# A block kernel's instruction order, written out anew, and a builder that keeps no times

## The chip, the cores and the metric

The kernel runs on one core of a Trainium2 chip. The metric is the device time of one execution in microseconds. The core has five instruction queues that run side by side and wait for each other through semaphores: PE (TensorE), ACT (ScalarE), DVE (VectorE), POOL (GpSimd) and SP (SyncE, which here only starts transfers).

## The reference

A transformer block with sliding-window attention and a gated MLP, both behind a layer norm that is modulated by a condition vector `c`. 2048 tokens, width 640, 32 heads of 20, window 256, MLP width 1536, all in bf16:

```python
mod = (silu(c) @ w_mod).reshape(1, 6, 1, -1)        # sa, ca, ga, sb, cb, gb
h = layernorm(x) * (1 + ca) + sa
q, k, v = heads(h @ wqkv)
p = softmax(where(0 <= i - j < 256, q @ k.T * 20 ** -0.5, -1e9))
x = x + ga * ((p @ v) @ wo)
h = layernorm(x) * (1 + cb) + sb
x = x + gb * ((sigmoid(h @ w_gate) * (h @ w_up)) @ w_down)
```

## The kernel before

The 2048 tokens are cut into eight blocks `a` of 256. For each block the program has these steps; the tag is the name that this document uses.

- `ln1`: load of x, layer norm (DVE statistics, a power on POOL, the normalisation on DVE or POOL), a transpose to `hT` (on PE for the first three blocks, by a transposing transfer on SP after that), and the modulation with scale and shift on DVE, ACT or POOL.
- `qkv`: q, k and v projections in 480-column pieces, five matmuls each. Copies on ACT or DVE bring them out of PSUM to `stg` (q, k) and `V`. q and k are then transposed to `QT` and `KT`, on PE for blocks 0 and 1 and by transfers on SP from block 2 on.
- `score_set`: scores of four heads at a time, one set after another into the one PSUM buffer `S` (four banks). ACT takes `exp` of them into `E` (L1015). A block has two halves of 16 heads, and a half has four "main" sets and one "edge" set (block 0 has other sets). POOL cuts the window's edges out of `E` (`masks`, L1040).
- `burst` and `norm`: the product with V (PV) for 16 heads into two PSUM tiles; DVE transposes them, divides by the row sums and transposes back. Eight small transfers write the result to a scratch tensor (`doc`), two read it back as `oT`.
- `outproj`: product with `wo`, the sum with x, the second layer norm, two transposing transfers to `h2T`, the modulation.
- `mlp`: gate and up products in pairs of 512 columns, tanh on ACT (L1209), the product `hh` on DVE (L1211), then the down projection, the sum with x, and the store.

The gates `ga` and `gb` are multiplied into `wo` (L1253) and `wd` (L1192) once; for each a row goes through a scratch tensor (`gate`) and is broadcast back to `gbc` by a transfer. The parts of `w_mod` first lie in the places of `wd`, `wu` and `hh`.

All matmuls but the small-tile ones are issued in one helper line (L668), the small-tile ones (scores, PV, the modulation rows) in another (L669). All products but the scores share four PSUM banks, `p_M`.

The order is not made by the program's text. Each of the 2121 operations gets a whole number from the table `PRIO`: divided by five it is the operation's rank in one common order, and the rest names its engine (0 PE, 1 ACT, 2 DVE, 3 POOL, 4 SP). `Prog.schedule` goes through the operations by rank, appends each to its engine's queue, gives each tile a buffer of its pool when its first operation comes, and `Prog.emit` writes the queues and the semaphore waits. Before, `schedule` also kept a model of times (start and end of each operation, of the transfers, of a port that DVE and POOL share), and took the buffer that by the model came free first:

```python
rts = [slot_time(t.pool, s + k) for k in range(step)]
if None not in rts and (best is None or max(rts) < best[0]):
    best = (max(rts), s)
```

Two tiles that are "mates" get neighbouring buffers.

Of the kernel before, what the change touches and what calls it, by code (L numbers as in the profile page):

```python
# [25 lines left out]
SWITCH = 0.095  # L26
ENGATTR = {"pe": "tensor", "act": "scalar", "dve": "vector", "pool": "gpsimd", "sp": "sync"}
ENGS = ("pe", "act", "dve", "pool", "sp")
OVERLAP = {"pe": 0.0, "act": 0.085, "dve": 0.075, "pool": 0.045, "sp": 0.0}
# [52 lines left out]
class Prog:  # L82
# [69 lines left out]
    def schedule(self):  # L152


        free = {e: START for e in ENGS}
        bw = 0.0
        lastturn = False
# [4 lines left out]
        pemode = 0  # L162
        portend = 0.0
        freed = {}

        def slot_time(pool, s):
            ten = pool.tenant[s]
            if ten is None:
                if not all(x.done for x in pool.init[s]):
                    return None  # L170
                return max([x.end + x.lat for x in pool.init[s]], default=0.0)
            return None if ten.left else freed[ten]
# [7 lines left out]
        for o in sorted(self.ops, key=lambda x: x.prio):  # L180
# [4 lines left out]
            st = max([o.tmin, free[e] + (SWITCH if e == "pe" and o.mode != pemode else 0.0)]  # L185
                     + [d.end + (0.0 if d.eng == "pe" and e == "pe" else d.lat) for d in o.deps])
            if o.isdma and e == "sp":
                st = max(st, bw - QMAX)
            for t in o.tiles:
                if t.slot is None:  # L190
                    step = 1 if t.mate is None else 2
                    best = None
                    for s in range(0, len(t.pool.tenant), step):
                        rts = [slot_time(t.pool, s + k) for k in range(step)]
                        if None not in rts and (best is None or max(rts) < best[0]):
                            best = (max(rts), s)
# [6 lines left out]
                for x in t.prev:  # L203
                    st = max(st, x.end + x.lat)
            if e == "dve" and o.port:
                st = max(st, free["pool"])
            elif e == "pool":
                st = max(st, portend)
            o.start = st
            if e == "pe":  # L210
                pemode = o.mout
            dur = o.dur[e]
            free[e] = st + dur - OVERLAP[e]
            if e == "dve" and o.port:
                portend = free[e]
            if o.isdma:
                turn = o.dlat > 3.0
                if e == "sp" and bw - st > 2.0:
                    free[e] += 0.35 if o.dur[e] > 1.0 else 0.1
                bw = max(st + o.dlat, bw + (MIXED if turn != lastturn and bw > st + o.dlat else 0.0)) + o.work  # L220
                lastturn = turn
                o.end = max(bw - 0.83, st + dur)
                s = rr
                rr = (rr + 1) % NDMA
                dmacnt[s] += 16
                o.key, o.val = f"d{s}", dmacnt[s]
                if dmalast[s] is not None:
                    o.deps.append(dmalast[s])
                dmalast[s] = o
            else:  # L230
                o.end = st + dur
# [16 lines left out]
        self.span = max(o.end for o in self.ops)  # L248
# [88 lines left out]
def c_pe(n):  # L337
# [3 lines left out]
PE_EPS = 0.14  # L341
PRIO = [
# [121 lines left out]
PQ = ()  # L464
KEEP = 3
DSAFE = 1.5
START = 0.8
PORTLAG = 0.05
MIXED = 0.55
NPB = 0  # L470
# [836 lines left out]
```

## Time and profile before

| | |
|---|---|
| median of 3 runs | 326.33 us (325.88 to 327.26) |
| span of the profiled execution, first to last instruction | 324.3 us |
| the profiled execution's own time | not listed; the three runs lie 1.6 to 3.0 us above the span |
| granted TensorE clock | 1.000 |
| PE, weight loads, DVE, ACT, POOL busy | 317.3, 222.7, 211.8, 212.3, 187.2 us |
| transfers | 37.85 MB, 117 GB/s over the span |

The row of a stretch has its bounds and length, then for PE, weight loads, DVE, ACT and POOL the busy time and the number of instructions, then the granted clock, the transfers' share and GB/s. A row of a timeline has its start, its length, the engine, the line, the operation, outputs and inputs, the count, and in brackets the idle time before it and what ended it. A row of the chain of waits has start, length and what ran or was waited for. PE's lengths overlap, since matmuls are pipelined: the next one starts before the last one's end.

### The profile page before, as it was taken

The page shows a single profiled execution, that of the slowest core. Times are in us where ns is not written, and L with a number is a line of the kernel's source. Part 1 is how long each engine was busy: PE and PEld are TensorE (multiplying, and loading weights), DVE is VectorE, ACT ScalarE, POOL GpSimd, SP SyncE. Part 2 cuts the span into 40 slices and gives each one's busy share as a digit, 9 for nine tenths or more (in the row PEclk, how much of TensorE's full clock was granted, in tenths as well). Part 3 has the DMA queues.
Part 4 walks back from the last instruction along what each step waited for, and adds up shares of the span by engine and source line. Part 5 has one row for each costly group of instructions (what it writes and reads, how often), then busy time and mean ns, then how long its engine had stood idle before and what let it go on. Part 6 is the DMA issues. An engine that isn't in the chain of part 4 may idle for free.

```text
span 324.3 us, 11594 instructions
## 1 busy us (share of the span) xinstructions
PE 317.3 (98%) x4872; PEld 222.7 (69%) x4873; DVE 211.8 (65%) x424; ACT 212.3 (65%) x316; POOL 187.2 (58%) x276
## 2 busy tenths in 40 slices
PE   8999999989999999999999999999999999999997
PEld 3564545446776568765776467877786788787885
DVE  5797898778687959674477475837463769264332
ACT  1899985889876687788687867786767764011120
POOL 5128869976668694847585939382939691012100
DMA  7998799989891383824405394340213032202101
GB/s 249 371 333 299 165 269 180 200 137 183 260 164 22 83 109 77 152 61 101 85 22 82 97 103 110 92 69 5 81 40 88 3 79 53 76 20 64 40 2 40
DMA packets 71694, 37.85 MB, mean 117 GB/s; under 512 B 45274, under 2 KB 70362, under 8 KB 71642
## 3 DMA queue, kind: packets, MB, share of 16 engines
q1 hardware_dynamic: 69616, 35.31, 48.3%
q10 hardware_dynamic: 2026, 1.80, 2.1%
q8 instruction: 38, 0.62, 0.8%
q14 instruction: 14, 0.11, 0.1%
HBM read 21.30 MB, written 5.25 MB: 82 GB/s over the span
## 4 chain that ended last, share of the span: by engine, by line
PE 73%; DMA 2%; SPq 2%; DVE 1%; POOL 1%; issue 0%; DVEq 0%
PE M L668 61%; PE S L669 6%; PE M L669 5%; DMA gbc<-gate 2%; SPq L803 2%; DVE wd L1192 1%; POOL x L793 0%; POOL st L788 0%; DVE hh L1211 0%; POOL E L1040 0%; DVE x L1230 0%; DVEq L310 0%
## 5 line engine op out<-in xcount | busy, mean ns | idle before, releaser
L1040 POOL TENSOR_SCALAR_AFFINE_SELECT E<-E 128x512 bf16<-128x512 bf16 (+1 forms) x176 | 142.6, 836 | 68.7 <-ACT E L1015 67.0
L1015 ACT ACTIVATE E<-S 128x512 bf16<-128x512 f32 (+2 forms) x184 | 150.9, 878 | 47.4 <-PE S L669 46.5
L668 PE MATMUL M<-wqkv,hT 128*128 128x480 bf16 (+1 forms) x340 | 73.9, 355 | 0.6 <-ACT hT L846 0.5
L668 PE MATMUL M<-h2T,wu 128*128 128x256 bf16 x480 | 68.0, 273 | 0.5 <-DVE hh L1211 0.5
L668 PE MATMUL M<-h2T,wg 128*128 128x256 bf16 x480 | 67.8, 273 | 0.0
L668 PE MATMUL M<-wd,hh 128*128 128x320 bf16 (+2 forms) x396 | 58.1, 295 | 0.0
L1209 ACT ACTIVATE sig<-M 128x512 f32<-128x512 f32 x48 | 28.9, 602 | 44.1 <-PE M L668 41.7
L1211 DVE SCALAR_TENSOR_TENSOR hh<-sig,M 128x512 bf16<-128x512 f32 x48 | 32.4, 681 | 37.1 <-ACT sig L1209 24.0
L668 PEld LDWEIGHTS M<-h2T,wu 128*128 128x128 bf16 x480 | 45.9, 98 | 8.4 <-issue 1.2
L668 PEld LDWEIGHTS M<-h2T,wg 128*128 128x128 bf16 x480 | 45.7, 98 | 7.1
L668 PEld LDWEIGHTS M<-wqkv,hT 128*128 128x128 bf16 x340 | 30.1, 98 | 27.6 <-DMA wqkv<-in_A_wqkv_dram 1.6
L668 PEld LDWEIGHTS M<-wd,hh 128*128 128x128 bf16 x396 | 36.8, 98 | 14.3 <-DVE hh L1211 0.2
L669 PEld LDWEIGHTS S<-QT,KT 20*64 20x64 bf16 (+1 forms) x1856 | 19.9, 100 | 21.3 <-ACT E L1015 12.0
L1230 DVE TENSOR_TENSOR x<-M,x 128x320 bf16<-128x320 f32 (+2 forms) x33 | 15.6, 476 | 27.2 <-PE M L668 27.2
L669 PE MATMUL S<-QT,KT 20*64 20x256 bf16 (+5 forms) x1856 | 32.1, 228 | 1.2 <-ACT E L1015 1.2
L776 DVE BATCH_NORM_STATS2 st<-x 128x6 f32<-128x320 bf16 x64 | 28.6, 477 | 2.3 <-DMA x<-in_A_x_dram 1.9
L1082 DVE STREAM_TRANSPOSE T<-M 128x512 f32<-128x512 f32 x32 | 21.5, 698 | 9.2 <-PE S L669 8.0
L668 PE MATMUL M<-wo,oT 128*128 128x320 bf16 x160 | 25.4, 299 | 0.0
L669 PE MATMUL M<-E,V 128*32 128x128 bf16 (+1 forms) x960 | 22.8, 246 | 0.8 <-ACT E L1015 0.4
L781 POOL TENSOR_SCALAR st<-st 128x2 f32<-128x2 f32 x16 | 3.7, 234 | 33.8 <-DVE st L778 33.6
L669 PEld LDWEIGHTS M<-E,V 128*32 128x32 bf16 x960 | 19.2, 97 | 5.3 <-issue 2.9
L1091 DVE STREAM_TRANSPOSE On<-Tn 128x1024 bf16<-128x1024 bf16 x16 | 19.8, 1240 | 0.3
(77 smaller groups left out, 240.2 us busy)
## 6 DMA issues: line engine op xcount, KB each, us to landing
x<-in_A_x_dram SPq DMA_DIRECT2D x23, 160.0 KB, 2.3
doc<-On SPq DMA_DIRECT2D x56, 40.0 KB
wd<-in_B_w_down_dram SPq DMA_DIRECT2D x4, 480.0 KB
wd<-in_w_mod_dram SPq DMA_DIRECT2D x5, 320.0 KB
wqkv<-in_A_wqkv_dram SPq DMA_DIRECT2D x4, 400.0 KB
wu<-in_w_mod_dram SPq DMA_DIRECT2D x5, 320.0 KB
oT<-doc SPq DMA_DIRECT2D x8, 192.0 KB, 2.5
out_dram<-x SPq DMA_DIRECT2D x9, 160.0 KB
```

The source lines that it names most:

```text
L668: return e.matmul(o, l, r, start=st, stop=sp, skip_group_check=True)
L669: return e.matmul(o, l, r, start=st, stop=sp, tile_position=tp, skip_group_check=True)
L776: A("dve", lambda e, g, bi=bi, j=j: e.bn_stats(v(bi * 12 + j * 6, 6), src[bi].ap[:, j * 320:(j + 1) * 320]), 0.48, reads=[src[bi].r()], wr ...
L781: A("pool", lambda e, g: e.tensor_scalar(v(28, n), var(), EPS, None, op0=ALU.add), 0.2, reads=[st.r(("m", bi)) for bi in range(n)], writes ...
L803: return e.dma_start_transpose(dst(), src())
L1015: A("act", lambda e, eng: e.activation(dst(), src(), ACT.Exp, scale=SM_SCALE), c_act(n), reads=[Sp.r()], writes=[E.r(key)], prio=3, tag=f" ...
L1040: A("pool", lambda e, eng: e.affine_select(rows(dst), rows(src), pattern=[[0, 8], [sign, n]], compare_op=ALU.is_ge, fill=0.0, base=base, c ...
L1082: A("dve", lambda e, g, h=h: e.transpose(T1.ap[:, 512 * h:512 * h + 512], X[h].ap), 0.694, reads=[X[h].r()], writes=[T1.r(h)], prio=3.5, t ...
L1091: A("dve", lambda e, g: e.transpose(On.ap[:], Tn.ap[:]), 1.22, reads=[Tn.r()], writes=[On.r()], prio=4, tag=f"tr2_{a}")
L1209: A("act", lambda e, g, pg=pg, sg=sg: e.activation(sg.ap[:], pg.ap[:], ACT.Tanh, scale=0.5), c_act(512), reads=[pg.r()], writes=[sg.r()], ...
L1211: A("dve", lambda e, g, pu=pu, sg=sg, f0=f0: e.scalar_tensor_tensor(out=hh.ap[:, f0:f0 + 2, :], in0=sg.ap[:].rearrange("p (a b) -> p a b", ...
L1230: A("dve", lambda e, g, ps=ps, bi=bi, c0=c0, n=n: e.tensor_tensor(x1[bi].ap[:, c0:c0 + n], ps.ap[:, 0:n], x1[bi].ap[:, c0:c0 + n], op=ALU. ...
```

## The change

`PRIO` has new numbers for all operations except those at the first 150 ranks. 98 operations change their engine: PE keeps its 907 operations and SP its 193; ACT has 335 in place of 333, DVE 427 in place of 424, POOL 259 in place of 264. The matmuls are the same, in another order.

`schedule` keeps no times any more. A buffer is chosen by the rank at which its last tenant's last operation stood, in place of the modelled time at which it came free; what the next tenant waits for is each engine's last operation by rank, in place of by modelled start. The two PSUM tiles of a PV burst are no longer mates (`TR1` is 2 here), so they may lie in any two banks.

```diff
-SWITCH = 0.095
-OVERLAP = {"pe": 0.0, "act": 0.085, "dve": 0.075, "pool": 0.045, "sp": 0.0}
...
-        free = {e: START for e in ENGS}
-        bw = 0.0
...
-        def slot_time(pool, s):
+        def slot_rank(pool, s):
             ten = pool.tenant[s]
             if ten is None:
-                if not all(x.done for x in pool.init[s]):
-                    return None
-                return max([x.end + x.lat for x in pool.init[s]], default=0.0)
+                return -1 if all(x.done for x in pool.init[s]) else None
             return None if ten.left else freed[ten]
...
-        for o in sorted(self.ops, key=lambda x: x.prio):
+        for rank, o in enumerate(sorted(self.ops, key=lambda x: x.prio)):
...
-                        rts = [slot_time(t.pool, s + k) for k in range(step)]
-                        if None not in rts and (best is None or max(rts) < best[0]):
-                            best = (max(rts), s)
+                        ranks = [slot_rank(t.pool, s + k) for k in range(step)]
+                        if None not in ranks and (best is None or max(ranks) < best[0]):
+                            best = (max(ranks), s)
...
                 if t.left == 0:
+                    freed[t] = rank
                     last = {}
-                    for x in t.ops:
-                        if x.isdma:
-                            last[x] = x
-                    for e2 in ENGS:
-                        xs = [x for x in t.ops if x.eng == e2 and not x.isdma]
-                        if xs:
-                            last[e2] = max(xs, key=lambda x: x.start)
+                    for x in sorted(t.ops, key=lambda x: x.prio):
+                        last[x if x.isdma else x.eng] = x
                     t.rel = list(last.values())
-                    freed[t] = max(x.end + x.lat for x in t.rel)
...
 PRIO = [
-    23, 28, 258, 8, 43, 33, 958, 18, 1448, 38, 3, 507, 513, 72, 67, 48, 53, 58, 76, 84, 101, 99, 144, 149, 154, 159,
+    23, 28, 258, 8, 43, 33, 773, 18, 958, 38, 3, 507, 513, 72, 67, 48, 53, 58, 76, 84, 101, 99, 144, 149, 154, 159,
...
         X = [Tile(p_M, f"O{a}_{q}x"), Tile(p_M, f"O{a}_{q}y")]
-        X[0].mate, X[1].mate = X[1], X[0]
+        if TR1 == 1:
+            X[0].mate, X[1].mate = X[1], X[0]
```

Around the places that matter later, the new order on SP has the four loads of `wd` among the first transfers (ahead of the first gate's broadcast and of the reading back of block 0), the bulk loads of the second halves of `wg` and `wu` behind the transposes of block 2's and 3's q and k, and the second gate's broadcast directly ahead of those bulk loads.

More of the change, by code (lines that the diff above doesn't have):

```diff
@@ L152, in schedule @@
     def schedule(self):
-        free = {e: START for e in ENGS}
-        bw = 0.0
-        lastturn = False
         order = {e: [] for e in ENGS}
@@ L161, in schedule @@
         rr = 0
-        pemode = 0
-        portend = 0.0
         freed = {}
-        def slot_time(pool, s):
+        def slot_rank(pool, s):
             ten = pool.tenant[s]
             if ten is None:
-                if not all(x.done for x in pool.init[s]):
-                    return None
-                return max([x.end + x.lat for x in pool.init[s]], default=0.0)
+                return -1 if all(x.done for x in pool.init[s]) else None
             return None if ten.left else freed[ten]
@@ L184, in schedule @@
             o.eng = e
[L185 to L188, printed above, removed]
             for t in o.tiles:
@@ L202, in schedule @@
                         take(t.mate, best[1] + 1 - t.odd)
[L203 to L215, printed above, removed]
-            if o.isdma:
[L217 to L223, printed above, removed]
-                rr = (rr + 1) % NDMA
[L225 to L231, printed above, removed]
+            if o.isdma:
+                dmacnt[rr] += 16
+                o.key, o.val = f"d{rr}", dmacnt[rr]
+                if dmalast[rr] is not None:
+                    o.deps.append(dmalast[rr])
+                dmalast[rr] = o
+                rr = (rr + 1) % NDMA
             order[e].append(o)
@@ L236, in schedule @@
                 if t.left == 0:
+                    freed[t] = rank
                     last = {}
-                    for x in t.ops:
-                        if x.isdma:
-                            last[x] = x
-                    for e2 in ENGS:
-                        xs = [x for x in t.ops if x.eng == e2 and not x.isdma]
-                        if xs:
-                            last[e2] = max(xs, key=lambda x: x.start)
+                    for x in sorted(t.ops, key=lambda x: x.prio):
+                        last[x if x.isdma else x.eng] = x
                     t.rel = list(last.values())
-                    freed[t] = max(x.end + x.lat for x in t.rel)
         self.order = order
-        self.span = max(o.end for o in self.ops)
     def emit(self):
@@ L338, in c_pe @@
     return max(n, 64) / 2400.0 + 0.0027
-PE_EPS = 0.14
 PRIO = [
[3 rows of a table removed]
[3 rows of a table added]
     92, 87, 187, 237, 242, 247, 253, 263, 272, 267, 280, 275, 290, 300, 305, 286, 317, 296, 322, 311, 376, 357, 386,
[1 row of a table removed]
[1 row of a table added]
     541, 495, 501, 665, 677, 480, 485, 491, 565, 570, 576, 545, 551, 630, 652, 525, 555, 561, 625, 660, 681, 685,
[111 rows of a table removed]
[111 rows of a table added]
 ]
@@ L466 @@
 DSAFE = 1.5
-START = 0.8
-PORTLAG = 0.05
-MIXED = 0.55
 NPB = 0
@@ L484 @@
 WSE = (("dve", "pool"), ("dve", "pool"))
-QMAX = 4.5
 WDT = 72.0
```

228 rows, old and new, of the table PRIO are left out of this document.

## The prediction

> **What bounds the kernel now.** I read the page first, then the busy time by stretches, then PE's timeline where a stretch is not full, then the chain of waits and the queues behind each gap.
>
> ```profile
> span 324.3 us, 11594 instructions
> PE 317.3 (98%) x4872; PEld 222.7 (69%) x4873; DVE 211.8 (65%) x424; ACT 212.3 (65%) x316; POOL 187.2 (58%) x276
> ...
> 0.00:10.00 10.00, 8.35 (x76) 4.11 (x77) 5.56 (x19) 2.62 (x6) 4.73 (x25) 1.00 0.81 269
> ...
> 30.00:40.00 10.00, 9.65 (x166) 5.63 (x164) 9.13 (x18) 9.56 (x17) 7.50 (x12) 1.00 0.64 172
> ...
> 60.00:70.00 10.00, 8.85 (x111) 4.00 (x108) 7.78 (x18) 9.29 (x15) 8.69 (x12) 1.00 0.92 180
> 70.00:80.00 10.00, 9.58 (x190) 6.19 (x189) 9.09 (x16) 8.21 (x14) 6.72 (x10) 1.00 1.03 171
> 80.00:90.00 10.00, 9.49 (x165) 7.91 (x168) 6.57 (x12) 8.66 (x15) 6.31 (x8) 1.00 0.82 253
> 90.00:120.00 30.00, 30.00 (x514) 19.60 (x503) 23.82 (x54) 20.89 (x30) 23.45 (x32) 1.00 0.47 87
> ```
>
> PE is busy for 317.3 of 324.3 us. From 90 us it has no idle time that shows (30.00 of 30.00). The changed kernel has the same 907 PE steps, with the same matmuls in them, so nearly all of this stays. An order can win only the gaps of the first 90 us and the price of changes between kinds of matmul. The first 10 us hold 1.65 us of idle, but the first 150 operations keep their places, so that is not in play. What is in play is 30 to 90 us; there ACT and DVE are close to full beside PE (9.56 and 9.13 of 10).
>
> PE's "busy" holds modelled ends, so I measure stalls from start to start. First the prices of PE work, and the place at 32 to 38 us:
>
> ```profile
> 32.42 0.40 PE L669 MATMUL S<-QT,KT 20*128 20x128 bf16 x16
> ...
> 38.23 0.84 PE L669 MATMUL M<-E,V 128*32 128x256 bf16 x32 [0.35 <-DVE hT L858]
> 39.00 1.19 PE L668 MATMUL M<-wqkv,hT 128*128 128x480 bf16 x5
> 40.12 0.43 PE L669 MATMUL S<-QT,KT 20*64 20x256 bf16 x24
> ...
> 42.99 3.21 PE L668 MATMUL M<-wqkv,hT 128*128 128x480 bf16 x15
> 46.13 0.43 PE L669 MATMUL S<-QT,KT 20*64 20x256 bf16 x24
> ...
> 33.61 4.23 POOL L1040 TENSOR_SCALAR_AFFINE_SELECT E<-E 128x1024 bf16<-128x1024 bf16 x4 [2.01 <-ACT E L1015]
> 37.08 1.45 DVE L858 TENSOR_SCALAR hT<-M,mA 128x256 bf16<-128x256 f32 x3
> ```
>
> Fifteen 480-wide matmuls up to a score set take 46.13 - 42.99 = 3.14 us, five take 40.12 - 39.00 = 1.12 us. So one costs (3.14 - 1.12) / 10 = 0.202 us, and what is left, 0.11 us, is the change of kind.
>
> Then the largest gap, 58 to 71 us, PE and the ACT work between:
>
> ```profile
> 58.92 0.41 PE L669 MATMUL S<-QT,KT 20*128 20x64 bf16 x32
> 59.27 1.39 PE L668 MATMUL M<-wqkv,hT 128*128 128x480 bf16 x6
> 60.49 0.84 PE L668 MATMUL M<-wo,oT 128*128 128x320 bf16 x5
> 61.60 0.43 PE L669 MATMUL S<-QT,KT 20*64 20x256 bf16 x24 [0.27 <-ACT E L1015]
> 61.96 0.58 PE L668 MATMUL M<-wqkv,hT 128*128 128x480 bf16 x2
> 62.38 0.84 PE L668 MATMUL M<-wo,oT 128*128 128x320 bf16 x5
> 63.06 0.77 PE L668 MATMUL M<-wqkv,hT 128*128 128x480 bf16 x3
> 64.13 0.43 PE L669 MATMUL S<-QT,KT 20*64 20x256 bf16 x24 [0.30 <-ACT E L1015]
> 64.66 2.82 PE L668 MATMUL M<-wqkv,hT 128*128 128x480 bf16 x12
> 67.91 0.43 PE L669 MATMUL S<-QT,KT 20*64 20x256 bf16 x24 [0.42 <-ACT E L1015]
> 68.26 1.79 PE L668 MATMUL M<-wqkv,hT 128*128 128x480 bf16 x8
> 70.48 1.50 PE L669 MATMUL M<-E,V 128*32 128x128 bf16 x64 [0.42 <-ACT E L1015]
> ...
> 59.49 2.06 ACT L1015 ACTIVATE E<-S 128x512 bf16<-128x512 f32 x4 [0.72 <-PE S L669]
> ...
> 63.97 2.07 ACT L811 ACTIVATE hT<-hT,mA 128x256 bf16<-128x256 bf16 x4
> ```
>
> There is one buffer of scores, S. A score set writes it, ACT takes the exponentials out, and only then may the next set start. With ACT free this cycle takes 2.53 us (61.60 to 64.13) for a main set and 2.68 us (58.92 to 61.60) for the edge set. Whatever PE has to do between two sets beyond that hides it; less leaves a stall. A 320-wide matmul costs 0.136 us (five from 62.38 to 63.06), a set 0.36 us (61.60 to 61.96). The four distances of this place against their work: 2.68 against 0.35 + 6 x 0.202 + 5 x 0.136 + 0.1 = 2.34; 2.53 against 0.36 + 5 x 0.202 + 5 x 0.136 + 0.1 = 2.15; 3.78 against 0.36 + 12 x 0.202 + 0.1 = 2.88 (here four modulations, 2.07 us, stand on ACT ahead of the exponentials); 2.57 against 0.36 + 8 x 0.202 + 0.1 = 2.08. Lost: 0.34 + 0.38 + 0.90 + 0.49 = **2.1 us**.
>
> The last gap, at 86 us, is a transfer's:
>
> ```profile
> 73.62 4.26 SPq L803
> 77.92 5.14 DMA gbc<-gate
> ...
> 85.72 0.69 DVE hh L1211
> ...
> 84.78 1.26 PE L668 MATMUL M<-h2T,wg 128*128 128x256 bf16 x10
> 86.54 1.25 PE L668 MATMUL M<-h2T,wu 128*128 128x256 bf16 x10 [0.51 <-DVE hh L1211]
> ```
>
> The broadcast of the second gate stood on SP behind a transpose whose issue took 4.26 us, and landed 5.14 us after its own start. The scaling of wd waited for it at the head of DVE's queue, the products hh behind that, and PE behind those: **0.5 us**.
>
> **The change part by part.** The builder without times gives no instruction another cost. It only fills the buffers by the rank at which they came free, and the two PV outputs of a burst need no longer be neighbours. 98 operations change their engine: ACT gets 2 operations more, DVE 3 more, POOL 5 fewer, which no full PE stretch notices.
>
> *Changes of kind.* Walking PE's order, I count 162 changes between full-array matmuls and the smaller tilings before, 159 after: 3 x 0.11 = **-0.3 us**. The Trainium skill (TensorEngine Tiling (Array Packing), Key Properties) says that changing the tiling mode drains TensorE; the 0.11 us above agree, and by that rule too fewer changes is a gain.
>
> *The score cycle at 50 to 71 us.* In the new order PE stands like this (matmuls between sets, from the program):
>
> ```
> edge set, wqkv 480 x10, main set, wo 320 x17, main set, wqkv 480 x4, wo 320 x3, wqkv 480 x6,
> main set, wqkv 480 x15, PV + main set, wqkv 480 x10, edge set, wqkv 480 x15, main set
> ```
>
> The distances are 0.35 + 10 x 0.202 + 0.1 = 2.47 us after the edge set (needs 2.68: 0.2 lost), 0.36 + 17 x 0.136 + 0.1 = 2.77, 0.36 + 10 x 0.202 + 3 x 0.136 + 0.1 = 2.89, 0.36 + 15 x 0.202 + 0.1 = 3.49, and more than that to the end of the stretch. All but the first are over 2.53. ACT now has two modulations in place of four before one set, and three copies before the next, where PE has 3.49 us of cover or more. So 2.1 becomes 0.2: **-1.9 us**. Bounds: -2.1 if the edge set finds ACT early, -1.0 if the copies that now stand before the exponentials are late themselves.
>
> *The second gate.* Its broadcast now stands on SP right after the transposes of block 2 and 3, where PE is near 60 us of its work and not near 70, and ten us of PE work lie between it and the first scaling of wd. Three quarters of wd's transfers go out before 40 us and the last before 50. The 0.5 us go: **-0.5**. If that cover failed too, it would be 0.
>
> *The second PV of block 0 (38.23 us before).* This gets tighter. Before, 38.23 - 32.42 = 5.8 us lie between the second score set and the PV; in that time the four masks on POOL take 4.23 us from 33.61 to 37.84, and the wait that ended last was a copy out of PSUM (hT, 0.48 us each of three). In the new order the PE work between them is 0.34 + 8 x 0.202 + 22 transposes of 128 columns at 0.202 x 128 / 480 = 0.054 + 0.8 for the modulation rows (20 of 320 columns, four at a time: 5 x 0.136 and a change) + a main set of 0.36 = 4.3, and with four more changes 4.7 us. The masks cannot end sooner than 33.61 - 32.42 + 4.23 = 5.4 us after the set. So 0.7 us are lost at the PV where 0.5 were, and the next score set is only 1.7 us of work behind the last one, on ACT's 2.53: together with the PSUM banks that the transposed copies hold I take **+0.5 us**, between 0 and +1.5. Three of block 1's transposes are now put in one row at 16 us, with one bank too few: **+0.2**, between 0 and 0.4.
>
> *The last transpose of K of block 2.* Its source leaves PE 6.7 us of PE work before the first score set of block 2 that reads it; before, 11.4 us. In between stand four edge exponentials and a copy on ACT, two transposes of hT on SP, and its own.
>
> ```profile
> 292.52 2.53 SPq L803 DMA_TRANSPOSE h2T<-x  x2
> ...
> 298.13 2.71 POOL L812 TENSOR_SCALAR h2T<-h2T,scB,shB 128x256 bf16<-128x256 bf16 x5 [6.48 <-issue]
> 302.10 1.15 PE L668 MATMUL M<-h2T,wu 128*128 128x256 bf16 x9
> ```
>
> An issue takes 2.53 / 2 = 1.27 us, and the reader of the second one started 298.13 - 293.79 = 4.3 us after that issue began. Counted from the end of the K chain on PE: ACT is held to 1.4 us by the edge set, the copy ends at 2.0, SP is free of hT's transposes at 2.7, landing at 7.0: 0.3 late, and 0.4 of stall elsewhere cover it. **+0.1**, between 0 and +4 (a jammed issue as at 73.62).
>
> *The end.* Before the last MLP, PE has, by the same prices, 11.1 us of work behind the last output projection in place of 13.9. The modulations that ran from 298.13 to 300.84 on POOL alone, 1.3 us ahead of need at 302.10, are now on ACT and POOL; the transposes go out later by one product. **+0.1**, 0 to +1. The last 6.5 us of down projection and the final stores stay.
>
> Sum: -0.3 - 1.9 - 0.5 + 0.5 + 0.2 + 0.1 + 0.1 = **-1.8 us**. The profiled span of 324.3 becomes 322.5. The three runs have a median of 326.33, 2.0 above the span; the same distance gives **324.5 us**. About 0.5% (1.6 us) is what a measurement of this kernel can tell from no change; the forecast lies just beyond it.
>
> **The rivals.** *The gain stays small.* ACT and DVE are at 9 of 10 from 30 to 50 us; work that they did in the gap at 60 now stands earlier, and four PSUM banks are shared by copies, PV and projections. If the place at 33 us costs its upper bound and the score cycle gains only 1.0: -0.3 - 1.0 - 0.5 + 1.5 + 0.4 + 0.1 + 0.1 = +0.3, so 326.0 to 326.6. For it: 9.56 and 9.13 of 10. Against it: from 42 us on each distance between sets is over its cycle but one.
>
> *Slower: SP's order.* SP issues in order. If one transpose ahead of K's last takes 4.26 us as at 73.62 instead of 1.27, that landing is 3.0 us later and stands 3.3 us behind PE. It decides from 6.7 us after the chain's end. Price +3.3 + the rest = -1.8 + 3.3 = +1.5, or 327.9; with a second one jammed 330. For it: the cover was nearly halved. Against it: the bulk loads of wg and wu have moved behind this point. The Trainium skill (TensorE: Matmul & The Clock Gate, part 1) says that an idle window of about 3.4 us takes the clock down to half; the granted clock was 1.00 in all rows here, and by that rule a stall of that length would cost up to 1.7 us more.
>
> *It does not do what it says:* 98 operations move, but the gaps only change places: 326.3, as for a small gain.
>
> **How the numbers follow.** The forecast gets 0.50 (its bounds, -1.0 to -3.2, mostly over 0.5%), small or no gain 0.27, SP's order and other new waits 0.23. The range goes from -3.5 (all bounds at their good end, and 0.5 us of the small waits) to +2.1: 322.8 to 328.4. The forecast's own range is 323.1 to 325.3. Faster by over 0.5% 0.50, within 0.27, slower 0.23.
>
> **What would show it.** PE near 9.9 of 10 in 60 to 90 us, no wait of S for E over 0.3 us there, no wait of wd's scaling for gbc, and a stall of about 1 us ahead of the second PV of block 0. A wait of a score set of block 2 for a transposed K, or PE under 9.4 in any ten us after 20, would prove it wrong.

## The result, and the profile after

The changed kernel is slower, by less than half a per cent. In the first comparison it takes 327.60 us (median of 6 runs, 326.83 to 328.36) against 326.11 us (6 runs, 325.86 to 327.26) of the kernel before; the ratio is 1.0048, with a 95% interval of 1.0032 to 1.0064. Two later comparisons gave 1.0027 (1.0013 to 1.0041) and 1.0025 (1.0014 to 1.0036). Forecast was 324.5 us.

The page of the kernel after, and its busy time by stretches: length of the stretch, then busy us and instructions of PE, PEld, DVE, ACT and POOL, then the granted clock, DMA share and GB/s. Line numbers are 45 or 46 lower than before (PE's L668 is now L622).

```profile
span 326.0 us, 11592 instructions
PE 316.8 (97%) x4872; PEld 222.4 (68%) x4873; DVE 216.5 (66%) x427; ACT 213.4 (65%) x318; POOL 183.6 (56%) x271
...
0.00:10.00 10.00, 7.83 (x76) 3.67 (x77) 5.44 (x18) 2.50 (x6) 4.72 (x25) 1.00 0.78 257
...
30.00:40.00 10.00, 9.31 (x166) 5.29 (x164) 9.44 (x21) 9.42 (x16) 7.34 (x9) 1.00 0.94 226
60.00:70.00 10.00, 10.00 (x177) 5.66 (x176) 9.52 (x24) 7.97 (x13) 8.56 (x13) 1.00 0.83 211
70.00:80.00 10.00, 8.92 (x129) 5.26 (x127) 7.49 (x15) 7.37 (x11) 7.28 (x10) 1.00 1.08 200
80.00:90.00 10.00, 10.00 (x201) 8.45 (x183) 7.56 (x14) 8.71 (x13) 6.44 (x8) 1.00 0.73 151
90.00:120.00 30.00, 29.88 (x470) 19.73 (x468) 24.66 (x54) 23.22 (x34) 21.23 (x29) 1.00 0.55 97
120.00:150.00 30.00, 29.63 (x530) 20.62 (x529) 21.19 (x37) 21.61 (x33) 20.49 (x31) 1.00 0.27 63
150.00:180.00 30.00, 29.27 (x538) 21.41 (x537) 18.33 (x32) 21.66 (x32) 18.89 (x26) 1.00 0.43 80
270.00:300.00 30.00, 29.08 (x292) 23.10 (x291) 16.20 (x31) 5.87 (x10) 3.97 (x8) 1.00 0.37 66
```

PE is busy for 316.8 us in place of 317.3, but idle for 9.2 in place of 7.0. Read against the rows of before, 60 to 70 and 80 to 90 us are now full: they had 1.15 and 0.51 us of idle. Three losses stand against that. From 70 to 80 us, 1.08 us are idle in place of 0.42. In the first 10 us, where both kernels run the same operations, it is 2.17 in place of 1.65. And the part behind 90 us, which I had taken to be full, has 0.12 + 0.37 + 0.73 + 0.92 = 2.1 us of idle in the four rows shown; before, each of the four had 30.00 of 30.00. The rows of the kernel before that the prediction does not show:

```profile
120.00:150.00 30.00, 30.00 (x518) 21.72 (x516) 22.20 (x39) 22.70 (x33) 18.30 (x25) 1.00 0.55 97
150.00:180.00 30.00, 30.00 (x562) 21.73 (x561) 17.95 (x34) 23.06 (x35) 20.79 (x29) 1.00 0.38 77
270.00:300.00 30.00, 30.00 (x255) 24.48 (x252) 16.04 (x32) 4.88 (x9) 2.81 (x6) 1.00 0.19 51
```

The late part is four places. The timeline of the kernel after, in order of time (start, busy us, engine, line, operation, out<-in; in brackets the idle time before it and what ended it):

```profile
129.73 0.60 PE L622 MATMUL M<-h2T,wg 128*128 128x256 bf16 x4
130.71 0.43 PE L622 MATMUL M<-wo,oT 128*128 128x320 bf16 x2 [0.37 <-DVE hh L1166]
...
127.00 1.71 DVE L1044 TENSOR_TENSOR Tn<-T,Dr 128x640 bf16<-128x640 f32 x1
128.74 1.25 DVE L1046 STREAM_TRANSPOSE On<-Tn 128x1024 bf16<-128x1024 bf16 x1
129.91 1.25 DVE L1166 SCALAR_TENSOR_TENSOR hh<-sig,M 128x512 bf16<-128x512 f32 x2
...
178.20 0.97 PE L622 MATMUL M<-wqkv,hT 128*128 128x480 bf16 x4 [0.73 <-DVE V L848]
...
175.92 0.67 DVE L1037 STREAM_TRANSPOSE T<-M 128x512 f32<-128x512 f32 x1
176.52 1.30 DVE L750 TENSOR_SCALAR x<-x,st 128x640 bf16<-128x640 bf16 x1
177.74 0.31 DVE L848 CAST V<-M 128x160 bf16<-128x160 f32 x1
...
277.50 0.34 ACTq L524 DMA_DIRECT2D out_dram<-x  x1
280.08 0.37 ACTq L524 DMA_DIRECT2D x<-in_A_x_dram  x1
280.50 1.09 ACT L765 ACTIVATE h2T<-h2T,shB,scB 128x256 bf16<-128x256 bf16 x2 [2.48 <-DMA out_dram<-x]
...
281.25 1.23 PE L622 MATMUL M<-h2T,wg 128*128 128x256 bf16 x8 [0.79 <-ACT h2T L765]
```

At 130 us the output projection (wo) needs a PSUM bank that the product hh empties. Its factors were there at 128.03 us, but hh stands on DVE behind the division (Tn) and the transpose (On) of another block, and starts at 129.91. At 177 us a projection needs the bank that the copy `V` empties; the copy stands behind a transpose and a layer-norm product. At 280 us two modulations are ready on ACT, but ahead of them stands the load of y14 into a buffer whose old content the store of 277.50 is still writing out: ACT stands still for 2.48 us, PE for 0.79. The fourth, 0.3 us at 289 us, is a store ahead of a scratch transfer on SP. Between the starts of PE's work, less the shortest distance for that work, the four cost 0.54, 0.89, 1.13 and 0.27 us: 2.8 us. These start-to-start stalls are meant where a stall is named below.

### The profile page after: what moved, and what is told of

It is laid out like the page before. It is cut to its first block, busy times and chain, and to the rows that moved or that the text cites. A ratio compares the mean times of both kernels' runs of the same rounds, so it can differ in the third digit from the quotient of the medians.

```text
span 326.0 us, 11592 instructions
## 1 busy us (share of the span) xinstructions
PE 316.8 (97%) x4872; PEld 222.4 (68%) x4873; DVE 216.5 (66%) x427; ACT 213.4 (65%) x318; POOL 183.6 (56%) x271
## 4 chain that ended last, share of the span: by engine, by line
PE 83%; DMA 6%; DVE 5%; SPq 1%; issue 1%; POOL 1%; ACT 1%; ACTq 0%; DVEq 0%
PE M L622 69%; PE S L623 8%; PE M L623 7%; DMA h2T<-x 3%; DMA wqkv<-in_A_wqkv_dram 2%; SPq L524 1%; DVE T L1037 1%; DVE x L750 1%; POOL E L994 1%; ACT E L969 1%; DVE wd L1147 1%; DMA out_dram<-x 1%; DVE hh L1166 1%; DVE h2T L766 0%; DVE On L1046 0%
## 5 line engine op out<-in xcount | busy, mean ns | idle before, releaser
L622 PE MATMUL M<-wqkv,hT 128*128 128x480 bf16 (+1 forms) x340 | 72.9, 355 | 2.3 <-issue 0.9
L622 PE MATMUL M<-h2T,wu 128*128 128x256 bf16 x480 | 70.4, 273 | 0.2 <-DVE h2T L766 0.2
L622 PE MATMUL M<-h2T,wg 128*128 128x256 bf16 x480 | 69.4, 273 | 0.8 <-ACT h2T L765 0.8
L622 PE MATMUL M<-wd,hh 128*128 128x320 bf16 (+2 forms) x396 | 57.9, 295 | 0.0
L622 PEld LDWEIGHTS M<-h2T,wg 128*128 128x128 bf16 x480 | 45.8, 98 | 8.5 <-issue 1.0
L622 PEld LDWEIGHTS M<-wqkv,hT 128*128 128x128 bf16 x340 | 30.3, 98 | 30.2 <-DMA wqkv<-in_A_wqkv_dram 2.0
L622 PEld LDWEIGHTS M<-h2T,wu 128*128 128x128 bf16 x480 | 45.5, 98 | 7.8 <-issue 0.3
L622 PEld LDWEIGHTS M<-wd,hh 128*128 128x128 bf16 x396 | 37.1, 98 | 15.0 <-DVE T L1037 0.2
L622 PE MATMUL M<-wo,oT 128*128 128x320 bf16 x160 | 27.0, 299 | 0.6 <-DVE hh L1166 0.4
L1119 DVE TENSOR_TENSOR x<-M,x 128x320 bf16<-128x320 f32 x32 | 15.3, 487 | 12.3 <-PE M L622 11.8
```

The lines of the kernel that those rows point to most:

```text
L622: return e.matmul(o, l, r, start=st, stop=sp, skip_group_check=True)
L1119: A("dve", lambda e, g, ps=ps, bi=bi, half=half: e.tensor_tensor(x1[bi].ap[:, half * 320:half * 320 + 320], ps.ap[:, 0:320], x1[bi].ap[:, ...
```

## The experiments

All kernels have the same TensorE steps with the same matmuls, but for the warm-up in three of them (p_shift, q_shift40 and r_all_shift40). Times are medians in us; "before" was run on the same chip, which is not the same for all rows, so that the ratios are the better measure between them.

| kernel | edit | time | before | ratio (95%) |
|---|---|---|---|---|
| a_same | none | 325.79 (one run) | 325.95 | |
| b_y14 | ACT: y14 behind the modulations | 326.09 | 325.95 | 1.0006 (0.9994 to 1.0019) |
| c_dve | DVE: three moves | 325.59 | 325.95 | 0.9986 (0.9973 to 1.0000) |
| d_all | b, c and the store on SP | 324.64 | 325.95 | 0.9965 (0.9952 to 0.9978) |
| a_again | none | 326.84 | 325.90 | 1.0027 (1.0013 to 1.0041) |
| e_oldorder | old order, new builder | 332.87 | 325.90 | 1.0212 (1.0191 to 1.0234) |
| f_new_old | new order, then old, new builder | 329.40 | 325.90 | 1.0112 (1.0091 to 1.0134) |
| p_shift | 190 PE instructions more ahead | 327.78 | 325.90 | 1.0061 (1.0039 to 1.0082) |
| i_before_nomate | before, without pairs of banks | 325.89 | 325.77 | 1.0004 (0.9989 to 1.0020) |
| k_neworder_oldslots | new order, old rule for buffers | 326.53 | 325.77 | 1.0016 (1.0005 to 1.0027) |
| q_shift40 | 40 PE instructions more ahead | 326.50 | 325.77 | 1.0022 (1.0009 to 1.0035) |
| r_all_shift40 | d_all and those 40 | 325.16 | 325.77 | 0.9981 (0.9970 to 0.9991) |
| a_third | none | 326.74 | 325.91 | 1.0025 (1.0014 to 1.0036) |
| s_loads | two weight loads later on SP | 330.58 | 325.91 | 1.0130 (1.0097 to 1.0162) |
| t_best | mends and those loads | 328.11 | 325.91 | 1.0064 (1.0042 to 1.0086) |
| u_new_old | new order, then old, old rule | 325.25 | 325.65 | 0.9994 (0.9980 to 1.0008) |
| v_old_new | old order, then new, old rule | 327.14 | 325.65 | 1.0043 (1.0030 to 1.0056) |
| w_mend4 | d_all without one exchange | 324.32 | 325.65 | 0.9960 (0.9946 to 0.9974) |

**The late waits.** My theory: the new order gained early as forecast and lost in four places behind 90 us. The rival: those places are the chance of one execution, or the loss is spread. The edits, as each queue's order. The names are the program's tags with the number of the block: `bmodu` is the modulation of h2T, `out` a store, `y14` a load of x, `tr2` the transpose On, `glu` a product hh, `bxh` a layer-norm product, `evv` a copy V, `amodu` the modulation of hT, `res1` the first sum with x, `n_ow` a transfer to the scratch tensor.

```diff
 ACT, 277 us (b_y14)
 bmodu6, out,
-y14, bmodu6, bmodu6
+bmodu6, bmodu6, y14
 DVE, 129, 177 and 94 us (c_dve)
-tr2_3, glu_1
+glu_1, tr2_3
-bxh3, evv7
+evv7, bxh3
-amodu5, res1_1
+res1_1, amodu5
 SP, 282 us (only in d_all and w_mend4; w_mend4 leaves the last exchange on DVE out)
-out, n_ow_7
+n_ow_7, out
```

> The changed kernel once more, nothing edited, to tell which of its stalls come from the order and which from one execution. Theory (queue order): the four late waits return at the same places with the same sizes within 0.2 us: 0.5 us ahead of wo2 at 130 us, 0.9 us ahead of projk6 at 177 us, 1.1 us in two steps ahead of mlpg6 at 280 us, 0.3 us ahead of wo7 at 289 us. Rival (chance of the profiled execution): they are gone or elsewhere, and the time is then 1 to 2 us nearer to the kernel before. Open on purpose: the 1.0 us break inside projv4 at 69.7 us, for which no semaphore is named, and the 0.5 us by which the same first 150 operations ran later from 11 us on. If they are of the program they return; if they are of the execution at least one of them moves by more than 0.3 us.

> The changed kernel, with the one load of y14 on ACT's queue put behind the two bmodu6 that stood behind it; everything else keeps its place. Theory (ACT's queue stood still while the load waited for the store to land): mlpg6 waits no longer at 280 us, 1.13 us are gone there, and the time falls from 327.6 to about 326.5 us (ratio to the kernel before 1.001). Rival 1 (bmodu6 was late for its own data): the stall stays over 0.8 us and the time with it, 327.6. Rival 2 (the stall only moves to the next wait, wo7 at 289 us, which waits for oT_7): less than half of it is gained, 327.1 or more.

> The changed kernel, with three moves on VectorE alone: glu_1 ahead of tr2_3 (130 us), evv7 ahead of bxh3 (177 us), res1_1 ahead of amodu5 (94 us). Theory (head of the line on VectorE): 0.54 + 0.89 + 0.19 = 1.6 us of TensorE stalls go, the time falls from 327.6 to about 326.0 (ratio 1.000). Rival 1 (the moved-back operations tr2_3, bxh3 and amodu5 are as urgent as those put ahead, so their users wait instead): the gain is under 0.6 us, 327.0 or more. Rival 2 (the banks were held by something else): the stalls at 130 and 177 us stay as they are.

> The changed kernel with the four moves of the two runs before it and one more, the store that stood on the SyncE queue ahead of the last n_ow_7 put behind it (289 us). Theory (the new order won 3.4 us between 30 and 90 us and lost 3.0 us again in single places after 90 us that nobody had counted): the mends add up, 1.13 + 1.62 + 0.27 = 3.0 us, the time is about 324.6 us and the ratio to the kernel before 0.995, faster than both kernels. Rival (the loss is spread, in prices of the order that show in no single stall): the mends bring under 1.2 us, 326.4 or more.

> The mended kernel once more, without the exchange of res1_1 and amodu5 at 94 us that cost as much as it won: y14 behind bmodu6 on ACT, glu_1 ahead of tr2_3 and evv7 ahead of bxh3 on VectorE, the store behind n_ow_7. Theory (the late waits are four places in the queues and nothing else): 1.1 us at 280 and 289 us and 1.4 us at 130 and 177 us less than the unedited kernel's 326.8, so 324.2 to 324.8 and a ratio of 0.995 to 0.9965, below both kernels. Rival (the 324.64 of the first mended kernel was luck with the break at 69 us): 325.2 or more.

The stalls at 130 and 177 us came back in a_same, a_again and a_third with 0.53 to 0.54 and 0.89 to 0.90 us, the one at 94 us with 0.19. The one at 280 us came back with 0.62 to 0.78 in place of 1.13; the one at 289 us did not come back. In the profile of c_dve, which is the fastest of its 12 runs, ACT stands still for 2.21 us at the same place and PE does not wait: what that costs PE depends on how early the transfers ahead of it land. The break inside projv4 was in some executions and not in others, and the start differed by some tenths; both are treated below.

With y14 moved, the stall at 280 us is gone; the median of 326.09 is 0.75 below a_again, which is what the stall cost in a_again (0.78). With the moves on DVE the stalls at 130 and 177 us are gone, and the median is 1.25 below. (a_again ran on another chip; b_y14, c_dve and d_all ran on one, and there d_all is 1.45 below b_y14 and 0.95 below c_dve.) The exchange at 94 us was a miss: in its place came two waits of 0.23 and 0.24 us. Together d_all came at 324.64, as expected, and w_mend4 on another chip at 324.32. The stretches of w_mend4 that answer to the losses:

```profile
120.00:150.00 30.00, 30.00 (x533) 20.98 (x531) 21.69 (x38) 22.26 (x32) 21.10 (x30) 1.00 0.29 67
150.00:180.00 30.00, 30.00 (x558) 21.92 (x563) 18.68 (x34) 22.56 (x34) 18.50 (x25) 1.00 0.41 76
270.00:300.00 30.00, 29.94 (x299) 23.85 (x297) 15.30 (x29) 6.59 (x12) 3.33 (x6) 1.00 0.35 68
```

They are full again but for 0.06 us (of the fourth place 0.22 us of stall are left, at 285 us), and the kernel is faster than both: 1.3 us below the kernel before, 2.2 (by the ratios) to 2.5 below the changed one (326.8). Three places, two on DVE and one on ACT, carry the whole verdict: without them the same order is faster than the old one. That is shown. The fourth was too small and too irregular to tell.

**Order or builder.** The change also fills buffers by rank in place of modelled time, and drops the pairing of banks. The four corners:

> The changed kernel unedited, timed against the kernel before on one chip, since its single run in the study before came at 325.8 us against 327.6 us first. Theory (the net of the order is a small gain, 2.8 us of stalls and 0.3 us of changes of kind won before 90 us against 2.0 us of new stalls behind it; on top lies a break of 1.0 us inside projv4 that only some executions have, and a start-up that varies by 0.5 us): the median is between 325.5 and 326.6, single runs spread over more than 1.2 us. Rival (the first comparison was right, the order is slower by 0.5 per cent): 327.0 or more, ratio 1.003 or more.

> The order of the kernel before, in the builder of the changed one (buffers taken by rank, the two output banks of a burst no longer taken as a pair). Theory (the builder is innocent, only the order counts): the same time as the kernel before within 0.3 us, ratio 0.999 to 1.001. Rival (buffers chosen by rank hand out banks that come free later): slower by 0.5 us or more.

> The kernel before, with one edit: the two output banks of a burst are no longer taken as a pair. The old order in the changed builder was 6.9 us slower, and that builder differs from the one before in two things, this pairing and the rule by which a free buffer is chosen (lowest rank of the operation that freed it, instead of the earliest modelled time). Theory (the rule is what costs): this kernel stays within 0.5 us of the kernel before, ratio 0.998 to 1.002. Rival (the missing pairs are what costs): 329 us or more.

> The new order, with the buffers chosen by modelled times as in the kernel before (no pairs): the fourth corner of order and rule. Theory 1 (by modelled time is the better rule for any order, since rank says nothing of when a bank comes free): the two waits for a bank at 130 and 177 us, 0.5 and 0.9 us, go or shrink, and the time falls below that of the changed kernel by 1 us or more, to 325.8 or less. Theory 2 (an order and its buffers are found together, and either one with the other's partner loses): slower than the changed kernel by 1 us or more, 328 or more. Between 325.8 and 328: neither.

The a_again median missed its interval by 0.24 us: the order is slower, by less than in the first comparison. That the builder is innocent was wrong. The old order loses 7 us in it, in waits like this one (timeline of e_oldorder; its lines are numbered 24 lower):

```profile
296.27 0.71 PE L598 MATMUL M<-h2T,wu 128*128 128x256 bf16 x5
298.52 0.61 PE L598 MATMUL M<-h2T,wg 128*128 128x256 bf16 x4 [1.55 <-DVE hh L1142]
```

A product of the MLP is given the bank that another product hh has still to empty. Rank says which operation stands earlier in the list, not which bank comes free earlier on another engine. The pairs cost nothing (i_before_nomate, 1.0004), so it is the rule. But the new order takes no harm from it: with the old rule it runs 326.53, and the waits at 130 and 177 us stay at 0.54 and 0.89. Neither theory of that run held. The loss of the change is the order's.

**Early gain and late loss apart.** Splices at 147 us, where the two orders have nearly the same operations behind them:

> A splice: the new order for its first 1115 operations, which is to about 147 us, and what is left in the old order. Theory (the new order is better before 90 us by 3.1 us, worse from 90 to 147 us by 0.7 us, worse behind that by 1.3 us): relative to the kernel before 3.1 - 0.7 = 2.4 us are won, less the break of 1.0 us in about half of the executions, so 323.6 to 324.6 us and a ratio of 0.992 to 0.996. Rival (gains before 90 us are given back later whatever the order is, since the old order waits for other things then): 325.5 or more.

> A splice that leaves the rule for buffers as it was: the new order for its first 1115 operations, to about 147 us, then the old order, both with buffers by modelled times and without pairs (that rule cost the old order nothing, 325.9 us, and the new order nothing, 326.5). Theory (the new order's gain lies before 90 us and its loss behind 120 us): 1.9 us of stalls and 0.3 us of changes of kind won by 90 us, 0.65 lost from 90 to 147 us, nothing lost behind, about 0.5 us of breaks and start-up that vary, so 324.5 to 325.3 and a ratio of 0.996 to 0.998. Rival (the late loss belongs to what was won early, whatever order follows): 326.0 or more.

> The reverse splice in the same builder: the old order for its first 1118 operations, then the new order. Theory: none of the early gain and the late waits at 177, 280 and 289 us alone, 0.9 to 1.4 us, so 326.7 to 327.4 and a ratio of 1.0025 to 1.0045. Rival (the late waits come only behind the new order's first part): 326.2 or less.

f_new_old told nothing of the order: its late half is the old order in the builder that costs it 1.5 us at 207 us, 0.9 at 264 and 1.7 at 293. With the old rule, v_old_new is slower by 0.43% and u_new_old is not: the median of 325.25 is in the interval expected, but its ratio of 0.9994 is not in the one expected (0.996 to 0.998), and is no gain that the measurement can tell. Nine of its 12 runs lie from 324.6 to 325.7, three at 326.6 to 326.7. So the loss lies in the late part, as far as the sign goes. The size is not clean: of v_old_new's stalls 0.89 us is the wait at 177 us, but 0.65 us at 156 and 159 us is of the seam, and the wait at 280 us was not there.

**The break at 69.7 us.** PE's timeline in the kernel after:

```profile
69.34 0.43 PE L623 MATMUL S<-QT,KT 20*64 20x256 bf16 x24
69.70 0.38 PE L622 MATMUL M<-wqkv,hT 128*128 128x480 bf16 x1
70.94 1.38 PE L622 MATMUL M<-wqkv,hT 128*128 128x480 bf16 x6 [0.86 <-issue]
```

It stops behind the first of five matmuls of one step (projv4, a v projection of block 4), with every input there since 68.03 us; no semaphore stands between the two. Of the transfers, one kind fits: the instruction queue q8 brings 16 KB at a time, 38 times in a run, which is once in 256 of PE's 9745 instructions.

```profile
q8 instruction: 38, 0.62, 0.8%
```

In the 13 executions with this code at this place, I set the start of the q8 transfer that comes last ahead of projv4 against projv4's own start. Neighbours are put together in one row:

| lead of the fetch on projv4 | break |
|---|---|
| 2.05 to 2.52 us (6 executions) | none |
| 1.99, 2.01 | none, 0.27 us |
| 1.91, 1.81 | 0.22, 0.43 |
| 1.59 | 0.53 |
| 1.26, 1.22 | 1.04, 1.11 |

The later the fetch, the longer the break, by about as much: in the six executions that have a break, PE goes on 2.33 to 2.53 us after the fetch began. That points to PE waiting for its own instructions, although the transfer itself had ended 1.4 to 1.6 us before PE went on; no record names what happens in between. Ahead of it lie 64 small matmuls and a score set, 88 matmuls with their weight loads in 1.8 us. Two attempts to get rid of it (the calls of matmul are shortened):

```diff
 warm-up on PE, five steps (p_shift: 21 and 48; q_shift40 and r_all_shift40: 6 and 170)
-for k in range(2): matmul(S, Eall[:, 0, 0:128], Eall[:, 0, 128:640])
+for k in range(21): matmul(S, Eall[:, 0, 0:32], Eall[:, 0, 128:176])
 SP (s_loads and t_best)
-gatebc, wu1, wg0, wg1, btr0, btr0, wu1, n_ow_1, wg1
+gatebc, wg0, btr0, btr0, wu1, wu1, n_ow_1, wg1, wg1
```

> The changed kernel with the first five steps on TensorE (they only keep it warm while the input is loaded) made of 21 small matmuls in place of 2 large ones, so that 190 more instructions lie ahead of everything else on TensorE. Theory (the break of 1.0 us inside projv4 is TensorE at the end of the code that it has fetched, 16 KB or 256 instructions at a time, where a dense stretch of 64 small matmuls and a score set lies just ahead of the fetch's end): the ends of the fetches now fall elsewhere, the break at projv4 does not come, the single runs spread less and their median is 0.3 to 0.7 us below that of the unedited kernel of this study. Rival 1 (the break comes of the transfers that land then, not of the code's place): it stays in some executions, median the same. Rival 2 (the break moves to another dense stretch): no break at projv4, one elsewhere, median the same.

> The changed kernel with 40 more instructions on TensorE ahead of everything (the warm-up made of 30 smaller matmuls in place of 10). With 190 more the break had moved by 66 instructions, from projv4 to the score set behind it, and 190 is 256 - 66: it sits at the end of a fetched 16 KB of code. That fetch begins in every run 3 to 4 us after TensorE has passed the place that asks for it, against about 1 us for most others, while 1.5 MB of weights are in the queues from 63.7 us on. Theory (the fetch is late since it stands behind those weights): with 40 more instructions it is asked for 2 us earlier, ahead of the weights, begins before 65 us, no break comes at 69 to 74 us, and the median is 0.3 to 0.8 us below 326.84. Rival (it is late for the code's place alone): the break stays, 40 instructions earlier in the program, and the median stays at 326.5 to 327.2.

> The kernel with the five mends (324.6 us) and the 40 additional instructions of the run before this one. Theory: the break of up to 1 us leaves those of its executions that had it, few by its spread of 323.9 to 324.8, so 324.3 to 324.6, ratio 0.995 to 0.9965, and no run over 325. Rival (the shift costs at the start or breaks elsewhere): 325.0 or more.

> The changed kernel unedited once more, beside the two edited ones on one chip, so that these can be held against it and not only against the kernel before. Both theories: 326.5 to 327.6 us (326.84 and 327.60 in the two comparisons so far), and stalls at 94, 130, 177 and 280 us as before.

> The changed kernel with two weight loads on the SyncE queue moved from 63.7 and 65.1 us to behind the two transposes of the MLP input (to about 72 us); TensorE first uses them at 84.7 us. TensorE's code and its place are unchanged. Theory (the fetch of code asked for at 64.4 us stands behind these weights, and so do the two transposes): the fetch begins before 66.5 us in place of 66.7 to 68.7, no break comes inside projv4 at 69.7, and the transposes land earlier, so that the stall of 0.3 to 0.7 us ahead of mlpu0 at 76 us goes as well; 0.7 to 1.2 us in the median. Rival 1 (the fetch is late for the code's place alone): the break stays in part of the executions, only the transposes gain, 0.2 to 0.5 us. Rival 2 (the loads now collide with the transposes and stores of 73 to 80 us): no gain.

> All that helped, in the new order: y14 behind bmodu6 on ACT, glu_1 and evv7 moved ahead on VectorE, the store behind n_ow_7, and the two weight loads behind the transposes; the exchange of res1_1 and amodu5 at 94 us is left out, since in the mended kernel it cost 0.47 us of new stalls (0.23 ahead of wo1, 0.24 ahead of down0) for the 0.19 that it took away. Theory (the gains add): 324.64 less 0.3 for that exchange, less 0.5 to 1.0 for the loads, so 323.3 to 323.9 us and a ratio of 0.992 to 0.994. Rival (as in the kernel with additional instructions, a wait comes in the place of the one removed): 324.4 or more.

With 190 instructions more, the break came 66 instructions later in the program (9 matmuls of projections and 24 of the score set behind projv4, each with its weight load); 190 + 66 is 256, a block. It ended 2.47 us after its fetch began, at 72.27. So it belongs to a block of code, and moved as such. That is rival 2, but the median was not the same: 327.78, 0.9 above a_again.

```profile
73.09 0.35 PE L623 MATMUL S<-QT,KT 20*128 20x64 bf16 x24
74.74 0.24 PE L623 MATMUL S<-QT,KT 20*128 20x64 bf16 x8 [1.29 <-issue]
```

With 40 more, the fetch began at 63.6 and no break came at 69 to 74 us, but the time gained little. The first score set of block 2 now waited 1.1 us (q_shift40):

```profile
65.78 0.43 PE L623 MATMUL S<-QT,KT 20*64 20x256 bf16 x24 [1.03 <-issue]
```

It started when the transposed K had landed, at 65.69 by the semaphore's updates, 5.0 us after that transfer's issue; in the kernel after it had been 3.3. The fetch fell among those transposes; that it delayed them was not tried. r_all_shift40 had the same 1.1 us, and lost 0.5 to d_all.

s_loads fell flat. The fetch still began at 67.4, with only one load of weights ahead of it: that it stands behind the weights was wrong. And the loads, now between the stores and transposes at 72 to 75 us, made the whole chain behind them late (SP's and PE's timelines of s_loads):

```profile
89.42 0.38 SPq L500 DMA_DIRECT2D oT<-doc  x1
89.84 0.41 SPq L500 DMA_DIRECT2D doc<-On  x1
92.08 0.37 SPq L500 DMA_DIRECT2D oT<-doc  x1
...
91.86 0.60 PE L598 MATMUL M<-h2T,wu 128*128 128x256 bf16 x4
94.71 0.98 PE L598 MATMUL M<-wo,oT 128*128 128x320 bf16 x5 [2.25 <-issue]
```

The last part of oT was issued at 92.08 in place of 88.08, and the output projection waited for it. It is the queue of my rival "SP's order", at another place: two issues put ahead cost 2.4 us there. Then the clock falls (rows of s_loads; the last three numbers are clock, DMA share and GB/s):

```profile
94.00:96.00 2.00, 1.29 (x8) 0.93 (x9) 1.97 (x6) 0.00 (x0) 0.56 (x1) 0.82 1.11 218
96.00:98.00 2.00, 2.00 (x32) 1.04 (x31) 2.00 (x7) 1.38 (x2) 0.00 (x0) 0.50 1.22 111
98.00:100.00 2.00, 2.00 (x14) 1.41 (x13) 1.32 (x4) 1.16 (x2) 0.78 (x2) 0.83 0.30 64
```

The trace has the granted clock at 0.50 for 3.41 us from 95.27 on, so PE's work there takes up to 1.7 us longer (an estimate, half of 3.41). Four of the six executions of s_loads have a mean clock of 0.995 and take 330.3 to 332.0 us; the two with 1.000 take 328.3 and 328.6. So s_loads lost by the wait and by the clock behind it. t_best has the same wait (2.5 us), and nine of its twelve executions have 0.995. It is under s_loads by 2.2 us among those with 1.000 and by 2.7 among those with 0.995, medians each, so the gains of the mends add up here too. Why this one fetch comes late stays open.

## Why the prediction was wrong, step by step

- *Score cycle, -1.9.* Right. The stalls of 2.1 us between 60 and 71 us are gone, 60 to 70 us went from 8.85 to 10.00, and no score set there waits for the exponentials; left is 0.14 us at the edge set, where I had 0.2.
- *Second gate, -0.5.* Right for the profiled execution (80 to 90 us went from 9.49 to 10.00). But the kernel before does not always pay it: the stall at 86 us was 0.68 in its profile, 0.49 in i_before_nomate and none in v_old_new. Of wd's four loads the new order has two ahead of the first gate's broadcast, not all, and they go out at 23.4, 38.6, 40.6 and 53.7 us, not three before 40 and the last before 50; since the scaling starts at 78.8 us, this changed nothing.
- *Second PV of block 0, +0.5.* Right: the idle time of 30 to 40 us rose from 0.35 to 0.69, and the PV at 37.68 waits 0.69 us where it waited 0.35, for the same copies.
- *Changes of kind, -0.3, and the bank at 16 us, +0.2.* Right in size: PE's work without stalls is 0.3 to 0.4 us less (by the usual distances between starts), and the transposes at 18.8 us wait 0.18. The 159 changes after are 156 between full-array matmuls and smaller tilings and three between two smaller tilings; no run has the changes alone. The Trainium skill (TensorEngine Tiling (Array Packing), Key Properties) has it that a change of tiling mode drains TensorE; fewer changes and less work agree.
- *K of block 2, +0.1.* Close to nothing, as forecast, but not as worked out: K landed at 63.65, 0.76 us ahead of its set at 64.41, and not 0.3 behind PE. With 40 PE instructions more it landed later and cost 1.1.
- *The end, +0.1.* No stall of PE over 0.12 us is left behind 290 us.
- *"From 90 us it has no idle time that shows ... so nearly all of this stays."* **This is the step that failed.** It is true of the old order. I carried it over to the new one without looking at its queues; for this stretch I had compared amounts of work and direct distances, not what stands at the head of DVE's, ACT's and SP's queues when PE needs something from behind it. There the new order lost 2.8 us in the first profile, and the mends brought 2.0 to 2.5.
- *No term at all* for what varies from run to run. The break cost 0 to 1.1 us. Nor is there one for the new order's first product of the MLP, at 76 us, which waits for the modulated h2T:

```profile
76.36 0.38 PE L598 MATMUL M<-h2T,wu 128*128 128x256 bf16 x2 [0.86 <-DVE h2T L742]
```

  That row is of w_mend4, which has no break and a stall of 0.92 us here; a_same and a_third, without a break too, have 0.68, and the profile of the changed kernel, with a break of 1.04, has 0.28. So the break costs only some 0.4 to 0.6 us in the end; the rest is waited for h2T anyway. The kernel before does not wait there. The first 10 us gave 2.17 us of idle in one profile and 1.91 in the next, and a_again alone waited 0.7 us at 34 us.
- *The distance from span to time.* I took 2.0 us from two unlike figures. In every execution that lists both it is 1.7 to 1.8 (327.72 for a span of 326.0), so the same sum would have said 324.2 to 324.3.

My own test in the prediction, PE under 9.4 in any ten us after 20, was met at 70 to 80 us (8.92), of the break (0.86) and the wait for h2T (0.22); without a break the row is still at 9.39 (a_same) and 9.14 (w_mend4). The forecast of 324.5 is close to what the same order takes with its late places mended (324.3 and 324.6): the early terms that it had were sized well, and the sum was made for a part of the kernel. That it comes so close is partly luck: the wait for h2T was missing on one side, and on the other the distance of 2.0 was 0.2 to 0.3 too long and a stall of 0.24 us at 48.66 us of the kernel before, which went as well, was left out. It is luck too that the rival "SP's order" named 327.9, close to 327.60: no transpose of block 2 was late in the changed kernel.

## What to carry to other kernels

A stretch that is full in the profile is full for its own order only. When a whole order is exchanged, walk each in-order queue over the full length and ask of every operation that frees a buffer or feeds the bound engine what long operation stands just ahead of it; a DMA issue on a compute engine's queue counts with the landing that it waits for. And change the order and the rule for buffers one at a time: this order took no harm from the rule, the old one lost 7 us by it.

## What was not expected of the hardware

PE seems able to run out of instructions: where small matmuls stand close (88 with their loads in 1.8 us), it stopped for 0.2 to 1.1 us with all inputs there (1.5 in p_shift), the longer the later its 16 KB of code had been fetched. No wait names it; the profile calls it "issue". One wait of 2.4 us of PE was followed by 3.41 us at half the granted clock (s_loads). And a transposing transfer's landing is no constant: the same K took 3.3 us from issue in one run and 5.0 in another.
